# Attention in segments: behind each score run either transposes or products with v

## Chip, cores and metric

The kernel runs on one core of one Trainium2 chip. The metric is the device time of one execution in microseconds (us); lower is better. The engines are called by their names in the profile: PE (TensorE, with PEld for its weight loads), DVE (VectorE), ACT (ScalarE), POOL (GpSimd) and SP (SyncE, whose queue issues the transfers).

## What is computed

The reference is attention with a bias from relative positions, and two feed-forward stages behind it. The change concerns the attention alone:

```python
B, H, S, D = q.shape                       # 4, 8, 576, 64
scores = scale * np.matmul(q, k.transpose(0, 1, 3, 2))
...
scores = scores + bias.transpose(2, 0, 1)[None, :, :, :]
scores = scores - np.max(scores, axis=-1, keepdims=True)
attn = np.exp(scores)
attn = attn / (np.sum(attn, axis=-1, keepdims=True) + 1e-09)
return np.matmul(attn, v).astype(np.float32)
```

Its output, 2304 tokens of 512 values, goes through `(h * cos(h)) @ w_out` with `h = x @ w_in`, then through a normalized gated stage. Those two stages are the same before and after the change.

## The kernel before

The order of the instructions is written out by hand: the schedule is manual, and each engine works through its own queue in program order. The program has three stretches. Up to about 60 us the bias is computed and stored. Up to about 308 us there is the attention. Then come the items of the two feed-forward stages (`run_item`), which use PE almost alone.

The attention is a loop over 16 units u, four batches b for each of four pairs of heads hp, and in each unit over five steps p (`step(u, p)`). A step p < 4 takes 128 queries of both heads, and p = 4 takes the last 64 queries of both heads at once. The work of one unit is:

- **Scores** (`qk`): each operand is split in two parts, and three products of parts make one score. For p < 4 the two heads lie on the two row halves of the array, which gives 12 matmuls on two PSUM tiles `psS`. For p = 4 there are 6 matmuls on one tile over all rows. `psS` has two buffers.
- **Softmax**: `most` (DVE) adds the bias, finds the largest score and writes `e` to SBUF. `exps` (ACT) makes the exponential in place and its sum. For the ninth tile (p = 4) a small POOL copy fills up 64 columns of `e` behind the exponential. `e` has three buffers, one for each step.
- **Transposes** (`tr`): `e` is transposed on PE in blocks of 128 columns into PSUM tiles `pt` (three buffers). ACT or DVE copies each tile into `eT` in SBUF. There is one `eT` for the first 256 queries (half 0) and one for the other 320 (half 1), each with one buffer. A step p < 4 has 9 transposes and p = 4 has 5.
- **Products with v** (`av`): for each half, five blocks c of keys, each with the two heads on the two column halves of the array, gathered in one PSUM tile `o` (one buffer). A product shows as two matmul records.
- **Normalization**: `recip` (DVE) inverts the sums, and a POOL copy widens them to `rw`. `norm` transposes `rw` on PE (two transposes) and copies the result to `rbc`. `norm_out` multiplies `o` by it (DVE), rounds it to `xh` (ACT) and stores the rest `xl` (POOL).

The units overlap. In step p of unit u the transposes belong to step p - 2 of the same unit, or to p + 3 of the unit before. The products belong to the unit before: half 0 at p = 0 (blocks 0 to 2) and p = 1 (blocks 3, 4), half 1 at p = 2 and p = 3. So PE runs scores, transposes and products in each of p = 0 to 3, and scores and transposes at p = 4. `recip` of half 1 stands at the end of p = 0 and its `rw` is transposed at p = 2. `recip` of half 0 stands at the end of p = 2 and its `rw` is transposed at p = 4. `norm_out` stands at the head of p = 2 and p = 4.

Side work goes along. `split_k` and `split_q` (POOL, a cast and a subtraction for each block) split the operands of the next unit: k at p = 2, blocks 0 and 1 of q at p = 3, blocks 2 and 3 at p = 4, and block 4 at p = 0 of the unit that uses it. From unit 4 on, `w_conv` (DVE, four quarters for each piece) and `w_tick` (ACT, POOL and the transfers) prepare weights for the later stages.

Of the kernel before, what the change touches and what calls it, by code (L numbers as in the profile page):

```python
# [7 lines left out]
F32 = mybir.dt.float32  # L8
# [7 lines left out]
B, H, S, D = 4, 8, 576, 64  # L16
# [15 lines left out]
WA = 1  # L32
WB = 6
# [21 lines left out]
def attn_moe(tc, qd, kd, vd, smallp, lrow, ident_d, wf1, wf2, rmsg, out):  # L55
    nc = tc.nc
# [23 lines left out]
    ident = const.tile([128, 128], F32, name="ident")  # L80
# [5 lines left out]
    psA, st_psA = pool("psA", space=PSUM, side="left")  # L86
# [96 lines left out]
    def load(u):  # L183
        for k, src in enumerate((kd, qd)):
            if u == 0:
                t = rawp.tile([128, 512, 2], I32, tag="raw", name="first", bufs=NRAW)
                t = t.rearrange("p a b -> p (a b)")[:, 0:640].bitcast(F32)
            else:
                t = prep.tile([128, 640], F32, tag="raw" + "kq"[k], name="raw" + "kq"[k], bufs=1)
            nc.sync.dma_start(t, src[u % 4, u // 4])  # L190
            raw_kq[u, k] = t
        if u == 0:
            kq[0] = [raw_kq[0, 0], raw_kq[0, 1]]
# [10 lines left out]
    def split_q(u, p):  # L204
        c = slice(128 * p, 128 * p + 128)
        two_parts(qt_[:, :, c], raw_kq[u, 1][:, c])
# [19 lines left out]
    ap, st_ap = pool("att")  # L226
# [3 lines left out]
    st = {}  # L230

    def qk(u, p):


        kt, qt = kq[u]
        terms = TERMS
        if u == 0:
            terms, kt, qt = ((0, 0),), kt.unsqueeze(1), qt.unsqueeze(1)
        pss = [psB.tile([128, 2, 512], F32, tag="S", name="psS", bufs=2) for _ in range(2 if p < 4 else 1)]
        for x in range(2):  # L240
            for n, (a, b_) in enumerate(terms):
                for hh, ps in enumerate(pss):
                    r = slice(64 * hh, 64 * hh + 64) if p < 4 else slice(0, 128)
                    k0 = 64 - 64 * hh + 288 * x
                    nc.tensor.matmul(ps[:, x, 0:288], qt[r, a, 128 * p:128 * p + 128], kt[r, b_, k0:k0 + 288],  # L245
                                     start=(n == 0), stop=(n == len(terms) - 1), tile_position=(64 * hh, 0))
        return pss

    def softmax(u, j, ps):
        most(u, j, ps)  # L250
        exps(u, j)
# [17 lines left out]
        if j == 8:  # L269
            nc.gpsimd.tensor_copy(e2[:, S:S + 64], e2[:, S - 64:S])  # L270

    def tr(u, p, first, spread=None):
        s_ = st[u]
        if first and p in (0, 2):
            s_["eT", p // 2] = ap.tile([128, 9, 256 + 32 * p], F32, tag=f"eT{p}", name=f"eT{p}", bufs=1)
        e = s_["e"][p]
        eT, q0 = s_["eT", min(p // 2, 1)], 128 * (p % 2 if p < 4 else 2)
        n = 128 if p < 4 else 64
        pt = psA.tile([128, 512], F32, tag="tr", name="pt", bufs=3)
        if first:  # L280
            for i in range(4):
                k0 = 128 * (i // 2) + (S + 64) * (i % 2) if p < 4 else 128 * i
                nc.tensor.transpose(pt[:, 128 * i:128 * i + 128], e[:, k0:k0 + 128], ident)  # L283
            nc.scalar.copy(eT[:, 0:512 // n, q0:q0 + n], pt.rearrange("p (c q) -> p c q", q=n))
            return
        if p < 4:
            for i in range(4):
                k0 = 128 * (2 + i // 2) + (S + 64) * (i % 2)
                nc.tensor.transpose(pt[:, 128 * i:128 * i + 128], e[:, k0:k0 + 128], ident)  # L289
            nc.vector.tensor_copy(eT[:, 4:8, q0:q0 + n], pt.rearrange("p (c q) -> p c q", q=n))  # L290
            pt = psA.tile([128, 512], F32, tag="tr", name="pt", bufs=3)
        nc.tensor.transpose(pt[:, 0:128], e[:, 512:640], ident)  # L292
        if spread is not None:
            norm(*spread, pt[:, 128:384])
        if p < 4:
            nc.scalar.copy(eT[:, 8, q0:q0 + n], pt[:, 0:128])
        else:
            for r in (slice(0, 64), slice(64, 128)):
                nc.vector.tensor_copy(eT[r, 8, q0:q0 + n], pt[r, r])
        del s_["e"][p]  # L300

    def av(u, half, cs):
        s_ = st[u]
        n = 256 if half == 0 else 320
        eT = s_["eT", half]
        if cs[0] == 0:
            s_["o"] = psA.tile([128, 512], F32, tag="o", name="o", bufs=1)
        o = s_["o"]
        if half == 1 and cs[0] == 0:
            for hh in range(2):  # L310
                nc.tensor.matmul(o[64 * hh:64 * hh + 64, 320:384], s_["r"][:, 8:9].to_broadcast([128, 64]),
                                 ident[:, 64 * hh:64 * hh + 64], start=True, stop=True, tile_position=(0, 64 * hh))
        vt = vts[u]
        for c in cs:
            for hh in ((0, 1) if c % 2 else (1, 0)):
                nc.tensor.matmul(o[64 * hh:64 * hh + 64, 0:n], vt[:, c, 64 * hh:64 * hh + 64],  # L316
                                 eT[:, 2 * c + (hh if c < 4 else 0), :], start=(c == 0), stop=(c == 4),
                                 tile_position=(0, 64 * hh))
# [3 lines left out]
    def recip(u, half):  # L322
        s_ = st[u]
        a, z = (0, 4) if half == 0 else (4, 9)
        nc.vector.tensor_scalar(s_["sum"][:, a:z], s_["sum"][:, a:z], 1e-9, None, op0=ALU.add)
        nc.vector.reciprocal(s_["r"][:, a:z], s_["sum"][:, a:z])
        s_["rw"] = ap.tile([128, 320], F32, tag="rbc", name="rw", bufs=2)
        nc.gpsimd.tensor_copy(s_["rw"][:, 0:256].rearrange("p (a b) -> p a b", b=64),
                              s_["r"][:, a:a + 4].unsqueeze(2).to_broadcast([128, 4, 64]))

    def norm(u, half, rp):
        s_ = st[u]
        rw = s_.pop("rw")
        for i in range(0, 256, 128):
            nc.tensor.transpose(rp[:, i:i + 128], rw[:, i:i + 128], ident)
        rbc = ap.tile([128, 320], F32, tag="rbc", name="rbc", bufs=2)
        nc.scalar.copy(rbc[:, 0:256], rp)
        s_["rbc", half] = rbc

    def norm_tail(u):  # L340
        s_ = st[u]
        nc.scalar.copy(s_["rbc", 1][:, 256:320], s_["o"][:, 320:384])

    def norm_out(u, half):
        hp, b = divmod(u, 4)
        s_ = st[u]
        n = 256 if half == 0 else 320
        rbc = s_["rbc", half]
        xt = ap.tile([128, 320], F32, tag="xt", name="xt", bufs=1)
        nc.vector.tensor_tensor(xt[:, 0:n], s_["o"][:, 0:n], rbc[:, 0:n], op=ALU.mult)  # L350
        t0 = b * S + 256 * half
        nc.scalar.copy(xh[:, hp, t0:t0 + n], xt[:, 0:n])
        nc.gpsimd.tensor_tensor(xl[:, hp, t0:t0 + n], xt[:, 0:n], xh[:, hp, t0:t0 + n].bitcast(F32), op=ALU.subtract)

    def start_unit(u):
# [6 lines left out]
            "m": sm[:, 0:9], "sum": sm[:, 10:19], "r": sm[:, 20:29], "e": {},  # L362
        }

    def step(u, p):
        hp, b = divmod(u, 4)
        if p == 0:
            start_unit(u)
        if u > 0 and p in (2, 4):
            norm_out(u - 1, p // 4)  # L370
        pss = qk(u, p)

        if p == 3 and u > 0:
            norm_tail(u - 1)
        back = (u, p - 2) if p > 1 else (u - 1, p + 3)
        if back[0] >= 0:
            tr(*back, True)
        for j, ps in enumerate(pss, 2 * p):
            softmax(u, j, ps)
            if b == 3:  # L380
                load_bias(hp + 1, j)
        if back[0] >= 0:
            tr(*back, False, (u, 0) if p == 4 else (u - 1, 1) if p == 2 and u > 0 else None)
        if p == 2:
            recip(u, 0)
        if p == 0 and u > 0:
            recip(u - 1, 1)
        if p < 4 and u > 0:
            av(u - 1, p // 2, ([0, 1, 2], [3, 4])[p % 2])
        if p == 0 and u > 1:  # L390
            split_q(u, 4)
        if 0 < u < 15:
            if p == 0:
                load(u + 1)
            if p == 2:
                split_k(u + 1)
            if p > 2:
                split_q(u + 1, 2 * p - 6)
                split_q(u + 1, 2 * p - 5)
        if u >= 4 and p != 2:  # L400
            if wstate["conv"] < wstate["absd"]:
                w_conv(1)
            if p == 4:
                w_tick(lambda i: i < WA + WB)

    ph0, st_ph0 = pool("ph0", side="right")
    L = ph0.tile([128, S], F32, name="L")
# [349 lines left out]
            w_fill(2 if n % 2 else 1)  # L757

    def rest():
        norm_out(15, 0)  # L760
        av(15, 1, [0, 1, 2, 3, 4])
        norm_tail(15)

    tr(15, 3, True)
    tr(15, 3, False)
    recip(15, 1)
    av(15, 0, [0, 1, 2, 3, 4])
    tr(15, 4, True)
    tr(15, 4, False, (15, 1))
    run_item(0, rest)  # L770
    run_item(1, lambda: norm_out(15, 1))
    st_psA.close()
# [79 lines left out]
```

## Time and profile before

| | |
|---|---|
| median of 3 runs | 1167.45 us (1166.16 to 1167.52) |
| the profiled execution's own time | 1166.25 us |
| its span, first to last instruction | 1164.5 us |
| PE busy | 1148.8 us |
| DVE, ACT, POOL busy | 811.5, 548.2, 442.5 us |

The profile is one execution. Busy time of PE is matmul time with modelled ends, so neighbours overlap by a little; the distance from start to start tells what a matmul takes in a row of its kind. An engine that is not the bottleneck may idle without cost.

### The profile page before, as it was taken

To read this page: it belongs to the slowest core of one execution; us is meant where nothing else is said; L and a number is where in the kernel's file an instruction comes from. 1 tells how busy PE (TensorE), PEld (TensorE's weight loads), DVE (VectorE), ACT (ScalarE), POOL (GpSimd) and SP (SyncE) were. 2 spreads that over 40 slices of the span, in tenths; PEclk is the share of its full clock that TensorE was granted. 3 is DMA by queue.
4 is the path that set the end of the run, shared out by engine and by line. 5 is a ranking of instruction groups with operands and counts; after the bars stand their busy time and mean duration, and the time that the engine had idled before them with its cause. 6 is when DMAs were issued, how large, how long until landed. Compare 5 with 4: busy or idle time off the path is not lost.

```text
span 1164.5 us, 18515 instructions
## 1 busy us (share of the span) xinstructions
PE 1148.8 (99%) x6962; PEld 912.8 (78%) x6962; DVE 811.5 (70%) x1524; ACT 548.2 (47%) x1122; POOL 442.5 (38%) x554
## 2 busy tenths in 40 slices
PE   7999999999999999999999999999999999999998
PEld 3477777777788888888888878888888888888887
DVE  8866678888698799698879897874655255543232
ACT  7977778888554454445444546332222232222111
POOL 0235556566242352244234356653321242133111
PEclk9999999999999999999999999999999999999999
DMA  6924343442111011111101100220112011100011
GB/s 217 315 79 149 105 145 117 144 148 78 33 55 55 1 55 55 37 37 55 55 19 55 37 19 19 59 69 19 43 54 68 1 55 55 55 1 1 37 55 72
DMA packets 30713, 79.27 MB, mean 68 GB/s; under 512 B 3872, under 2 KB 4128, under 8 KB 30624
## 3 DMA queue, kind: packets, MB, share of 16 engines
q1 hardware_dynamic: 30480, 77.80, 21.1%
q8 instruction: 55, 0.90, 0.3%
q10 hardware_dynamic: 144, 0.29, 0.1%
q14 instruction: 34, 0.28, 0.1%
HBM read 62.47 MB, written 15.61 MB: 67 GB/s over the span
## 4 chain that ended last, share of the span: by engine, by line
PE 87%; DVE 8%; ACT 3%; issue 1%; DMA 1%; SPq 0%; POOL 0%; DVEq 0%; ACTq 0%
PE y L552 25%; PE h L552 14%; PE hg L552 12%; PE hv L552 12%; PE o L316 7%; PE psS L245 7%; PE pt L283 4%; PE pt L289 2%; PE psb L475 2%; ACT G L484 1%; DVE yacc L655 1%; PE pt L292 1%; DVE t L592 1%; DVE sq L671 1%; DVE w L128 1%
## 5 line engine op out<-in xcount | busy, mean ns | idle before, releaser
L602 POOL TENSOR_TENSOR g<-t,g 128x512 fp32r<-128x512 f32 (+1 forms) x80 | 98.4, 1230 | 234.5 <-ACT g L601 234.5
L619 POOL TENSOR_TENSOR g<-t,g 128x512 fp32r<-128x512 f32 (+1 forms) x60 | 74.4, 1240 | 292.1 <-ACT g L618 292.1
L259 DVE CUSTOM_DVE_ANT_0 e<-psS,bias 128x576 f32<-128x576 f32 x144 | 104.0, 755 | 52.0 <-PE psS L245 49.8
L552 PE MATMUL y<-g,wB 128*128 128x512 f32 (+1 forms) x600 | 133.4, 370 | 1.3 <-DVE yacc L655 1.2
L614 DVE TENSOR_TENSOR t<-t,hg 128x512 f32<-128x512 f32 (+1 forms) x60 | 38.0, 633 | 137.5 <-ACT t L613 137.5
L552 PEld LDWEIGHTS y<-g,wB 128*128 128x128 f32 x600 | 105.0, 188 | 21.6 <-DVE yacc L655 2.5
L613 ACT ACTIVATE t<-hg 128x512 f32<-128x512 f32 (+1 forms) x60 | 33.2, 554 | 167.3 <-PE hg L552 161.0
L618 ACT CAST g<-t 128x512 fp32r<-128x512 f32 (+1 forms) x60 | 34.7, 578 | 164.3 <-DVE t L617 164.3
L268 ACT ACTIVATE e<-e,sm 128x576 f32<-128x576 f32 x144 | 110.7, 773 | 1.2 <-DVE sm L259 1.2
L552 PE MATMUL h<-xh,wB 128*128 128x512 f32 (+1 forms) x360 | 109.1, 369 | 0.0
L552 PE MATMUL hg<-xh,wB 128*128 128x512 f32 (+1 forms) x320 | 96.9, 368 | 0.4 <-DVE t L614 0.4
L552 PE MATMUL hv<-xh,wB 128*128 128x512 f32 (+1 forms) x320 | 97.1, 369 | 0.0
L596 ACT ACTIVATE r<-r 128x512 f32<-128x512 f32 (+1 forms) x80 | 47.1, 589 | 106.0 <-DVE r L593 105.7
L601 ACT CAST g<-t 128x512 fp32r<-128x512 f32 (+1 forms) x80 | 46.2, 578 | 96.8 <-DVE t L600 87.6
L552 PE MATMUL y<-wB,g 128*128 128x512 f32 x378 | 91.4, 389 | 0.0
L316 PE MATMUL o<-eT,v 128*64 128x256 f32 (+1 forms) x640 | 90.5, 413 | 0.0
L245 PEld LDWEIGHTS psS<-kt,qt 64*128 64x128 f32 (+1 forms) x810 | 62.0, 185 | 29.4 <-issue 20.3
L552 PEld LDWEIGHTS y<-wB,g 128*128 128x128 f32 x378 | 70.5, 188 | 14.3
L245 PE MATMUL psS<-kt,qt 64*128 64x288 f32 (+1 forms) x810 | 79.8, 309 | 0.4 <-DVE sm L259 0.4
L552 PE MATMUL y<-g,wC 128*128 128x512 f32 (+1 forms) x360 | 79.8, 370 | 0.1
L617 DVE TENSOR_TENSOR t<-t,hv 128x512 f32<-128x512 f32 (+1 forms) x60 | 38.0, 633 | 58.5 <-PE hv L552 58.4
L552 PEld LDWEIGHTS h<-xh,wB 128*128 128x128 f32 x360 | 65.8, 188 | 12.1 <-issue 0.5
(136 smaller groups left out, 2663.7 us busy)
## 6 DMA issues: line engine op xcount, KB each, us to landing
raw<-in_wf_dram SPq DMA_DIRECT2D x68, 512.0 KB, 3.6
bdram<-G SPq DMA_DIRECT2D x36, 295.5 KB, 4.8
bias<-bdram SPq DMA_DIRECT2D x32, 288.0 KB, 4.3
v<-in_vd_dram SPq DMA_DIRECT2D x16, 320.0 KB, 4.7
rawk<-in_kd_dram SPq DMA_DIRECT2D x15, 320.0 KB, 5.0
rawq<-in_qd_dram SPq DMA_DIRECT2D x15, 320.0 KB, 3.6
out_dram<-yacc SPq DMA_DIRECT2D x16, 256.0 KB, 2.0
bias<-bdram SPq DMA_DIRECT2D x4, 144.0 KB, 2.9
```

Of the source, the lines that this page charges most:

```text
L245: nc.tensor.matmul(ps[:, x, 0:288], qt[r, a, 128 * p:128 * p + 128], kt[r, b_, k0:k0 + 288], start=(n == 0), stop=(n == len(terms) - 1), t ...
L259: nc.vector.tensor_tensor_reduce(out=e.rearrange("p (a b) -> p a b", a=2), in0=ps[:, :, 0:288], in1=bias_t[j].rearrange("p (a b) -> p a b" ...
L268: nc.scalar.activation(e, e, AF.Exp, bias=s_["m"][:, j:j + 1], scale=-1.0, accum_out=s_["sum"][:, j:j + 1])
L283: nc.tensor.transpose(pt[:, 128 * i:128 * i + 128], e[:, k0:k0 + 128], ident)
L316: nc.tensor.matmul(o[64 * hh:64 * hh + 64, 0:n], vt[:, c, 64 * hh:64 * hh + 64], eT[:, 2 * c + (hh if c < 4 else 0), :], start=(c == 0), s ...
L552: nc.tensor.matmul(ps, a, b_, start=(first and k == 0), stop=(last and k == tot - 1))
L596: nc.scalar.activation(r, r, AF.Abs)
L601: nc.scalar.copy(g[:, 0, :tn], t)
L602: nc.gpsimd.tensor_tensor(g[:, 1, :tn], t, g[:, 0, :tn].bitcast(F32), op=ALU.subtract)
L614: nc.vector.tensor_tensor(t, t, pg, op=ALU.mult)
L617: nc.vector.tensor_tensor(t, t, pv, op=ALU.mult)
L619: nc.gpsimd.tensor_tensor(g[:, 1, :tn], t, g[:, 0, :tn].bitcast(F32), op=ALU.subtract)
```

## The change

`step` is written anew. Behind the scores of p = 0, 2 and 4 stand only transposes, and behind those of p = 1 and 3 only products with v:

- p = 0: all transposes of steps 3 and 4 of the unit before (w = u - 1), and of its `rw` of half 1 (`turn_end`);
- p = 1: all products of half 1 of w, and its `norm_out`;
- p = 2: all transposes of steps 0 and 1 of u, and of its `rw` of half 0;
- p = 3: all products of half 0 of u, and its `norm_out`;
- p = 4: all transposes of step 2 of u.

`tr` becomes `blocks` (four transposes into one `pt`) and `ninths` (the ninth blocks of up to two steps, and `rw`, in one `pt`). They return their copies, which `step` puts between the exponentials. `norm` goes into `ninths`. `recip` of half 1 moves from the end of p = 0 to the end of p = 4, behind the `split_q` of that step, and `recip` of half 0 from p = 2 to p = 1. The weight quarters move from one each at p = 0, 1, 3 and 4 to two each at p = 1 and p = 3, and `w_tick` from p = 4 to p = 1. The places of `split_k` and `split_q` stay.

```diff
--- before.py
+++ after.py
@@ -269,49 +269,59 @@
         if j == 8:
             nc.gpsimd.tensor_copy(e2[:, S:S + 64], e2[:, S - 64:S])
 
-    def tr(u, p, first, spread=None):
+    def blocks(u, p, k):
         s_ = st[u]
-        if first and p in (0, 2):
+        if k == 0 and p in (0, 2):
             s_["eT", p // 2] = ap.tile([128, 9, 256 + 32 * p], F32, tag=f"eT{p}", name=f"eT{p}", bufs=1)
         e = s_["e"][p]
         eT, q0 = s_["eT", min(p // 2, 1)], 128 * (p % 2 if p < 4 else 2)
         n = 128 if p < 4 else 64
         pt = psA.tile([128, 512], F32, tag="tr", name="pt", bufs=3)
-        if first:
-            for i in range(4):
-                k0 = 128 * (i // 2) + (S + 64) * (i % 2) if p < 4 else 128 * i
-                nc.tensor.transpose(pt[:, 128 * i:128 * i + 128], e[:, k0:k0 + 128], ident)
-            nc.scalar.copy(eT[:, 0:512 // n, q0:q0 + n], pt.rearrange("p (c q) -> p c q", q=n))
-            return
-        if p < 4:
-            for i in range(4):
-                k0 = 128 * (2 + i // 2) + (S + 64) * (i % 2)
-                nc.tensor.transpose(pt[:, 128 * i:128 * i + 128], e[:, k0:k0 + 128], ident)
-            nc.vector.tensor_copy(eT[:, 4:8, q0:q0 + n], pt.rearrange("p (c q) -> p c q", q=n))
-            pt = psA.tile([128, 512], F32, tag="tr", name="pt", bufs=3)
-        nc.tensor.transpose(pt[:, 0:128], e[:, 512:640], ident)
-        if spread is not None:
-            norm(*spread, pt[:, 128:384])
-        if p < 4:
-            nc.scalar.copy(eT[:, 8, q0:q0 + n], pt[:, 0:128])
-        else:
-            for r in (slice(0, 64), slice(64, 128)):
-                nc.vector.tensor_copy(eT[r, 8, q0:q0 + n], pt[r, r])
-        del s_["e"][p]
-
-    def av(u, half, cs):
+        for i in range(4):
+            k0 = 128 * (2 * k + i // 2) + (S + 64) * (i % 2) if p < 4 else 128 * i
+            nc.tensor.transpose(pt[:, 128 * i:128 * i + 128], e[:, k0:k0 + 128], ident)
+        to = eT[:, 4 * k:4 * k + 512 // n, q0:q0 + n]
+        return lambda copy: copy(to, pt.rearrange("p (c q) -> p c q", q=n))
+
+    def ninths(u, ps, half=None):
+        s_ = st[u]
+        pt = psA.tile([128, 512], F32, tag="tr", name="pt", bufs=3)
+        for i, p in enumerate(ps):
+            nc.tensor.transpose(pt[:, 128 * i:128 * i + 128], s_["e"].pop(p)[:, 512:640], ident)
+        if half is not None:
+            rw = s_.pop("rw")
+            for i in range(0, 256, 128):
+                nc.tensor.transpose(pt[:, 256 + i:384 + i], rw[:, i:i + 128], ident)
+
+        def out(copy):
+            if ps[0] == 0:
+                copy(s_["eT", 0][:, 8, 0:256], pt[:, 0:256])
+            else:
+                q0 = 128 * (ps[0] - 2)
+                copy(s_["eT", 1][:, 8, q0:q0 + 128], pt[:, 0:128])
+
+        def small(copy):
+            for r0 in (0, 64):
+                r = slice(r0, r0 + 64)
+                copy(s_["eT", 1][r, 8, 256:320], pt[r, 128 + r0:192 + r0])
+
+        def spread():
+            rbc = ap.tile([128, 320], F32, tag="rbc", name="rbc", bufs=2)
+            nc.scalar.copy(rbc[:, 0:256], pt[:, 256:512])
+            s_["rbc", half] = rbc
+        return out, small, spread
+
+    def av(u, half):
         s_ = st[u]
         n = 256 if half == 0 else 320
         eT = s_["eT", half]
-        if cs[0] == 0:
-            s_["o"] = psA.tile([128, 512], F32, tag="o", name="o", bufs=1)
-        o = s_["o"]
-        if half == 1 and cs[0] == 0:
+        o = s_["o"] = psA.tile([128, 512], F32, tag="o", name="o", bufs=1)
+        if half == 1:
             for hh in range(2):
                 nc.tensor.matmul(o[64 * hh:64 * hh + 64, 320:384], s_["r"][:, 8:9].to_broadcast([128, 64]),
                                  ident[:, 64 * hh:64 * hh + 64], start=True, stop=True, tile_position=(0, 64 * hh))
         vt = vts[u]
-        for c in cs:
+        for c in range(5):
             for hh in ((0, 1) if c % 2 else (1, 0)):
                 nc.tensor.matmul(o[64 * hh:64 * hh + 64, 0:n], vt[:, c, 64 * hh:64 * hh + 64],
                                  eT[:, 2 * c + (hh if c < 4 else 0), :], start=(c == 0), stop=(c == 4),
@@ -327,15 +337,6 @@
         s_["rw"] = ap.tile([128, 320], F32, tag="rbc", name="rw", bufs=2)
         nc.gpsimd.tensor_copy(s_["rw"][:, 0:256].rearrange("p (a b) -> p a b", b=64),
                               s_["r"][:, a:a + 4].unsqueeze(2).to_broadcast([128, 4, 64]))
-
-    def norm(u, half, rp):
-        s_ = st[u]
-        rw = s_.pop("rw")
-        for i in range(0, 256, 128):
-            nc.tensor.transpose(rp[:, i:i + 128], rw[:, i:i + 128], ident)
-        rbc = ap.tile([128, 320], F32, tag="rbc", name="rbc", bufs=2)
-        nc.scalar.copy(rbc[:, 0:256], rp)
-        s_["rbc", half] = rbc
 
     def norm_tail(u):
         s_ = st[u]
@@ -362,46 +363,84 @@
             "m": sm[:, 0:9], "sum": sm[:, 10:19], "r": sm[:, 20:29], "e": {},
         }
 
+    def turn_end(u, *now):
+        a, b, c = blocks(u, 3, 0), blocks(u, 3, 1), blocks(u, 4, 0)
+        out, small, spread = ninths(u, (3, 4), 1)
+        a(nc.scalar.copy)
+        if now:
+            exps(now[0], 0)
+        c(nc.scalar.copy)
+        b(nc.vector.tensor_copy)
+        out(nc.scalar.copy)
+        small(nc.vector.tensor_copy)
+        if now:
+            exps(now[0], 1)
+        spread()
+
+    def convert(n):
+        for _ in range(n):
+            if wstate["conv"] < wstate["absd"]:
+                w_conv(1)
+
     def step(u, p):
         hp, b = divmod(u, 4)
+        w = u - 1
         if p == 0:
             start_unit(u)
-        if u > 0 and p in (2, 4):
-            norm_out(u - 1, p // 4)
-        pss = qk(u, p)
-
-        if p == 3 and u > 0:
-            norm_tail(u - 1)
-        back = (u, p - 2) if p > 1 else (u - 1, p + 3)
-        if back[0] >= 0:
-            tr(*back, True)
-        for j, ps in enumerate(pss, 2 * p):
-            softmax(u, j, ps)
+        for j, ps in enumerate(qk(u, p), 2 * p):
+            most(u, j, ps)
             if b == 3:
                 load_bias(hp + 1, j)
-        if back[0] >= 0:
-            tr(*back, False, (u, 0) if p == 4 else (u - 1, 1) if p == 2 and u > 0 else None)
-        if p == 2:
+        if p == 0:
+            turn_end(w, u)
+            if u > 1:
+                split_q(u, 4)
+            if u < 15:
+                load(u + 1)
+        elif p == 1:
+            if w >= 0:
+                av(w, 1)
+            exps(u, 2)
+            exps(u, 3)
+            if u >= 4:
+                convert(2)
+                w_tick(lambda i: i < WA + WB)
             recip(u, 0)
-        if p == 0 and u > 0:
-            recip(u - 1, 1)
-        if p < 4 and u > 0:
-            av(u - 1, p // 2, ([0, 1, 2], [3, 4])[p % 2])
-        if p == 0 and u > 1:
-            split_q(u, 4)
-        if 0 < u < 15:
-            if p == 0:
-                load(u + 1)
-            if p == 2:
+            if w >= 0:
+                norm_tail(w)
+                norm_out(w, 1)
+        elif p == 2:
+            cs = [blocks(u, i, k) for i in range(2) for k in range(2)]
+            out, _, spread = ninths(u, (0, 1), 0)
+            cs[0](nc.scalar.copy)
+            cs[1](nc.scalar.copy)
+            exps(u, 4)
+            cs[2](nc.vector.tensor_copy)
+            cs[3](nc.vector.tensor_copy)
+            out(nc.scalar.copy)
+            exps(u, 5)
+            spread()
+            if 0 < u < 15:
                 split_k(u + 1)
-            if p > 2:
-                split_q(u + 1, 2 * p - 6)
-                split_q(u + 1, 2 * p - 5)
-        if u >= 4 and p != 2:
-            if wstate["conv"] < wstate["absd"]:
-                w_conv(1)
-            if p == 4:
-                w_tick(lambda i: i < WA + WB)
+        elif p == 3:
+            av(u, 0)
+            exps(u, 6)
+            exps(u, 7)
+            if u >= 4:
+                convert(2)
+            norm_out(u, 0)
+        else:
+            c0, c1 = blocks(u, 2, 0), blocks(u, 2, 1)
+            out, _, _ = ninths(u, (2,))
+            c0(nc.scalar.copy)
+            exps(u, 8)
+            c1(nc.vector.tensor_copy)
+            out(nc.scalar.copy)
+        if 0 < u < 15 and p > 2:
+            split_q(u + 1, 2 * p - 6)
+            split_q(u + 1, 2 * p - 5)
+        if p == 4:
+            recip(u, 1)
 
     ph0, st_ph0 = pool("ph0", side="right")
     L = ph0.tile([128, S], F32, name="L")
@@ -757,16 +796,10 @@
             w_fill(2 if n % 2 else 1)
 
     def rest():
-        norm_out(15, 0)
-        av(15, 1, [0, 1, 2, 3, 4])
+        av(15, 1)
         norm_tail(15)
 
-    tr(15, 3, True)
-    tr(15, 3, False)
-    recip(15, 1)
-    av(15, 0, [0, 1, 2, 3, 4])
-    tr(15, 4, True)
-    tr(15, 4, False, (15, 1))
+    turn_end(15)
     run_item(0, rest)
     run_item(1, lambda: norm_out(15, 1))
     st_psA.close()
```

## Rows read from the trace of the kernel before

**Rows 1.** The page, part 1: busy us, share of the span and instructions.
```profile
PE 1148.8 (99%) x6962; PEld 912.8 (78%) x6962; DVE 811.5 (70%) x1524; ACT 548.2 (47%) x1122; POOL 442.5 (38%) x554
```
**Rows 2.** Busy us by stretch: length, PE, PEld, DVE, ACT, POOL, granted clock, DMA, GB/s.
```profile
124.00:301.00 177.00, 177.00 (x1580) 127.79 (x1577) 142.59 (x370) 141.32 (x372) 102.13 (x191) 1.00 0.36 116
301.70:304.60 2.90, 2.85 (x24) 2.22 (x23) 2.37 (x5) 2.59 (x7) 1.22 (x2) 1.00 0.01 3
```
**Rows 3.** Chain of waits in order of time: start, us, what; scores of p = 4.
```profile
252.87 0.99 PE psS L245 x6
...
300.95 0.99 PE psS L245 x6
```
**Rows 4.** Timeline of PE: start, us, line, operation, tiles, shapes, count.
```profile
236.78 1.06 PE L245 MATMUL psS<-kt,qt 128*128 128x288 f32 x6
237.68 0.60 PE L283 MATMUL pt<-ident,e 128*128 128x128 f32 x4
...
238.98 1.07 PE L245 MATMUL psS<-kt,qt 64*128 64x288 f32 x12
239.97 0.65 PE L283 MATMUL pt<-ident,e 128*128 128x128 f32 x4
240.46 0.60 PE L289 MATMUL pt<-ident,e 128*128 128x128 f32 x4
240.90 0.27 PE L292 MATMUL pt<-ident,e 128*128 128x128 f32 x1
241.10 1.52 PE L316 MATMUL o<-eT,v 128*64 128x256 f32 x12
242.55 1.05 PE L245 MATMUL psS<-kt,qt 64*128 64x288 f32 x12
...
304.56 2.38 PE L316 MATMUL o<-eT,v 128*64 128x256 f32 x20
306.87 0.66 PE L283 MATMUL pt<-ident,e 128*128 128x128 f32 x4
```
**Rows 5.** Timeline of DVE and ACT at a step p = 4.
```profile
237.88 0.76 DVE L259 CUSTOM_DVE_ANT_0 e<-psS,bias 128x576 f32<-128x576 f32 x1 [0.30 <-PE psS L245]
...
238.37 0.58 ACT L284 COPY eT<-pt 128x512 f32<-128x512 f32 x1 [0.29 <-PE pt L283]
...
238.86 0.78 ACT L268 ACTIVATE e<-e,sm 128x576 f32<-128x576 f32 x1
...
239.53 0.19 ACT L268 ACTIVATION_READ_ACCUMULATOR e<-e,sm 128x1 f32 x1
```
**Rows 6.** Groups by line and form, 60 to 308 us: busy us, mean ns, idle before.
```profile
L328 POOL COPY rw<-sm 128x256 f32<-128x256 f32 x31 | 12.6, 405 | 33.3 <-DVE sm L326 33.3
...
L353 POOL TENSOR_TENSOR xl<-xt,xh 128x256 fp32r<-128x256 f32 x15 | 11.0, 733 | 41.7 <-ACT xh L352 41.7
...
L325 DVE TENSOR_SCALAR sm<-sm 128x5 f32<-128x5 f32 x16 | 7.8, 489 | 0.0
...
L350 DVE TENSOR_TENSOR xt<-o,rbc 128x256 f32<-128x256 f32 x15 | 6.4, 425 | 0.5
...
L352 ACT CAST xh<-xt 128x256 fp32r<-128x256 f32 x15 | 6.0, 401 | 0.7
...
L326 DVE RECIPROCAL sm<-sm 128x5 f32<-128x5 f32 x16 | 3.1, 191 | 0.6
```
**Rows 7.** Timeline of POOL, from the copy of e on.
```profile
239.79 0.35 POOL L270 COPY e<-e 128x64 f32<-128x64 f32 x1 [0.76 <-ACT e L268]
240.08 0.29 POOL L196 CAST qt<-rawq 128x128 fp32r<-128x128 f32 x1
...
240.86 0.29 POOL L196 CAST qt<-rawq 128x128 fp32r<-128x128 f32 x1
...
241.64 1.28 POOL L149 TENSOR_TENSOR wB<-w,wB 128x512 fp32r<-128x512 f32 x1
```
**Rows 8.** One line, 60 to 308 us: duration in ns, min/median/max, first and last start.
```profile
L197 POOL TENSOR_TENSOR qt<-rawq,qt x70: 453/458/847, 75.7 to 291.4; 128x128 fp32r<-128x128 f32 x70
```

## The prediction

> **What bounds the kernel now.** I read the page's busy times first. TensorE (PE) is busy for 1148.8 of 1164.5 us, so only PE time counts, unless a wait is put into its order [rows 1]. Then the table by stage: in the steady part of the attention (124 to 301 us) PE is busy all the time at the full granted clock (1.00, the level of 2.4 GHz), with VectorE (DVE) at 142.6, ScalarE (ACT) at 141.3 and GpSimd (POOL) at 102.1 of 177 us [rows 2]. Then the chain of waits in order of time: it stays on PE, and the scores of p = 4 start three units apart at 252.87 and 300.95, which makes 16.03 us a unit [rows 3]. The last view is PE's timeline, which shows what fills those 16.03 us: score runs (S), runs of transposes (T) and runs of products with v (A), each a little longer than its matmuls [rows 4].
>
> The price of a run, from [rows 4]. Four transposes inside a T run take 240.90 - 240.46 = 0.44, so 0.109 each. The first four take 0.49 (0.05 for entering) and the last one 0.20 up to the first product (0.09 for leaving): a T run costs 0.109 for each transpose and a constant of 0.15. Only the T run behind p = 4 enters free (11 transposes, 237.68 to 238.98, 1.30, constant 0.10). For A, 12 matmul records of 256 columns take 1.45 and 20 take 2.31, so a pair takes 0.215 and the constant is 0.16; I use 0.15, the T constant, for both. An S run takes 0.99, and 0.90 at p = 4.
>
> **What the change takes away.** Work on PE is the same: 45 transposes and 20 products (40 records) a unit, 5 S runs. The number of runs falls. Before, T follows each of five S runs and A follows four of the T runs: 9 runs of T or A. After, T stands behind p = 0 (16 transposes), p = 2 (20) and p = 4 (9), A behind p = 1 and p = 3: 5 runs. Two T constants and two A constants go: 4 x 0.15 = 0.60 us a unit. The S runs keep theirs, whatever stands next to them. This holds for units 1 to 15; unit 0 has as many changes of kind as before, and the last stretch before the first item of the next stage comes out about even when its waits are followed through. 15 x 0.60 = 9.0 us.
>
> S directly before A does not occur in the trace. Its lowest price is that of any other change (0.15, already counted in the run), its highest that of the S-to-T and T-to-A changes which it replaces, one constant more. Then 2 x 0.15 a unit come back and the gain is 4.5 us. I take the low price: the two constants that the trace has, of T behind S and of A behind T, are nearly the same. The Trainium skill (TensorEngine Tiling (Array Packing), Key Properties) says that changing the tiling mode drains TensorE. By that rule S to A is one drain like the others, which is the low price, and the sum is the same.
>
> Smaller edits: three ACT copies of 128 columns where there were four (one of them twice as wide), and the conversion quarters moved from four steps to two. ACT and DVE have 20% of the steady part free [rows 2], so these count as nothing; if that cover went, PE would see it only where a product run waits for a copy. Followed through p = 0 to p = 3 with durations like those of [rows 5, 6], the copies come at least 0.1 us ahead of the run that needs them, and the transposes' three PSUM buffers are freed in time. The DMA issues are as many as before and go ahead of their use by several steps.
>
> **What the change adds: a wait on POOL.** Before, the widened reciprocals rw of unit u-1 were made at p = 0 and transposed at p = 2. Now recip(u, 1) stands at the end of p = 4, and its transposes close the T run of the next p = 0. POOL works in the order written, and between the last products of unit u and this rw stand ten POOL instructions: the subtraction xl of norm_out(u, 0), moved to p = 3; split_q for blocks 0 and 1; the small copy of e behind exps(u, 8); split_q for blocks 2 and 3. Then rw. norm_out(u, 0) cannot start before the last product of p = 3. (split_k, at p = 2, is done by then.)
>
> I set the start of the p = 4 scores to zero. The products' records end 0.07 after the next S starts [rows 4]. DVE's product takes 0.425, ACT's cast 0.401, the subtraction 0.733 [rows 6]; a hand-over between engines takes 0.07, as from ACT's last record (239.53 + 0.19) to POOL's copy at 239.79 [rows 5, 7]. So xl ends at 0.07 + 0.07 + 0.425 + 0.07 + 0.401 + 0.07 + 0.733 = 1.84. Two split_q take 241.64 - 240.08 = 1.56 [rows 7], so 3.40. The copy of e holds POOL for 240.08 - 239.79 = 0.29, so 3.69; its own input is ready earlier: most(u, 8) starts 1.10 after S4's start and takes 0.76 (236.78 and 237.88), the ACT copy ahead of exps starts 0.69 after T's start, at 1.59, exps follows 0.49 later and its last record ends 0.86 after that, at 2.94 [rows 4, 5]. Two more split_q: 5.25. rw takes 0.405 [rows 6]: 5.66, and 0.07 to PE: 5.73.
>
> PE without a wait: S4 0.90, nine transposes 9 x 0.109 + 0.10 = 1.08, S0 0.99, then 14 transposes, 14 x 0.109 + 0.05 = 1.58: the transposes of rw are due at 4.55. They come 5.73 - 4.55 = 1.18 us late. Part of it is spent sooner: the scores of p = 0 need split_q's block 0, which ends at about 1.84 + 0.78 + 0.07 = 2.69, and were due at 1.98, so PE waits about 0.7 there and about 0.5 at rw. Behind rw on PE everything is queued, S of p = 1 first. split_q is issued in p > 2 only for 0 < u < 15, so 14 units pay: 14 x 1.18 = 16.5 us.
>
> Bounds of this stall. Below: the pitch from xl to the next POOL instruction could be 0.05 shorter than its duration, as the copy's is, which gives 1.13; nothing in the order written lets rw pass the eight split instructions, so I see no reason for less than 0.85, a quarter below. Above: one of the four subtractions slowed from 0.458 to 0.847, its median and its maximum in the attention [rows 8], gives 1.57.
>
> **Sum.** -9.0 + 16.5 = +7.5 us on the profiled run, whose own time is 1166.25 (span 1164.5): 1173.8. The median of the runs shown is 1.2 higher, 1167.45, which gives 1175.0. I predict 1174, between the low end of the stall and this sum.
>
> **Rivals.**
> *Faster: POOL is not late.* The place is the head of S0 and the end of T at p = 0. It decides below a stall of 9.0 / 14 = 0.64 us a unit, so the POOL chain would have to be 0.5 us shorter than the 5.7 that I add up. For it: the page itself calls POOL's spans rough. Against: the 1.56 are start to start, in a stretch where POOL never idled. If POOL were on time, DVE would be next: recip waits for exps(u, 8) (2.94), then takes 0.489 and 0.191 [rows 6], so most(u+1, 0) would start at about 3.65 and the second one end at 3.65 + 2 x 0.76 = 5.17, where S1 was due at 2.97 + 16 x 0.109 + 0.15 = 4.86. That is a stall of 0.3 a unit, 4.5 us in all, and 1166.25 - 4.5 = 1161.7 (1163 by the median). With no stall at all: 1157.3 (1158.5).
>
> *No change.* The stall lies near break-even, 0.5 to 0.8: 1165 to 1170. It needs the chain to be 0.4 to 0.7 shorter than added up.
>
> *Slower still.* S to A costs twice and a subtraction of POOL is slowed in each unit: -4.5 + 14 x 1.57 = +17.5, 1184.
>
> *The clock falls.* From 301.7 to 304.6 PE did little but transposes, with gaps, and the granted clock stayed at 1.00 [rows 2]. If it fell to half behind each of the three T runs for one S run, 3 x 0.99 x 15 = 45 us would be lost: 1211. The Trainium skill (TensorE: Matmul & The Clock Gate, Part 4) says that transposes do not count as busy for the clock in the way matmuls do. By that rule the longer T runs speak for this rival; the trace, with 1.00 through its densest stretch of transposes, does not bear it out.
>
> **How the numbers follow.** Forecast, a stall of 0.85 to 1.5 (1170 to 1180): 0.68. Slower still: 0.08. The clock: 0.02. No change: 0.08. Faster: 0.14. About 0.2% is what a measurement of this kernel can tell from no change, 2.3 us. That gives slower 0.78, same 0.08, faster 0.14. The likeliest case alone spans 1170 to 1180. The range reaches down to 1163, the faster case with DVE's wait, and up to 1183; about 0.08 lie below it and 0.04 above.
>
> **What would show it.** In the profile after: S runs of p = 0 and p = 1 whose weight loads wait for POOL, together about 1.2 us a unit; POOL without a pause from xl to rw; 16.6 us from one p = 4 to the next; five T and A runs a unit with unbroken 16 and 20 transposes, and 20 records of products; no wait of PE on the eT copies; the clock at 1.00. The prediction is wrong if rw's transposes follow the other fourteen at 0.109, if S0 starts 0.20 behind the last transpose of p = 4, or if PE waits for DVE or ACT at the product runs instead.

## The result, and the profile after

The changed kernel takes 1173.68 us (median of 6 runs, 1172.76 to 1174.08); the kernel before, measured beside it, 1166.85 us. The ratio is 1.0059 with a 95% interval of 1.0049 to 1.0070: slower by about 7 us. The forecast was 1174. The profiled execution took 1173.41 us with a span of 1171.6 us, 7.1 more than before.

The table by stage of the kernel after (length, then busy us of PE, PEld, DVE, ACT and POOL, the granted clock, DMA):

```profile
124.00:301.00 177.00, 171.49 (x1521) 125.22 (x1519) 135.91 (x357) 137.37 (x348) 97.26 (x191) 1.00 0.37 114
```

In [rows 2] PE was busy in all of these 177 us; now it idles for 5.5 of them by its records, and the clock is as it was. The waits from 76 to 310 us (who waited for whom: us in total, times, longest) say for what:

```profile
PEld pt L294 <- POOL rw L338: 8.2, 14, 0.6
...
PEld psS L245 <- DVE sm L335: 6.9, 14, 0.5
...
PEld psS L245 <- POOL qt L196: 5.3, 14, 0.4
...
PEld psS L245 <- POOL qt L197: 3.4, 14, 0.2
```

Each stands 14 times. In the three that name POOL, the transposes of rw wait for its copy, and the scores of p = 0 wait for both halves of a split_q block. The one that names DVE (`recip`) stands at the scores of p = 2 and costs PE nothing: the scores there start at 254.11, 0.08 before the record of the products in front of them ends (251.32 + 2.87), as scores behind products do in [rows 4] (0.07). So an idle weight load need not be a loss, and these sums are more than PE's own loss. The loss is read from PE's timeline, from one p = 4 through the next p = 1:

```profile
240.93 1.06 PE L245 MATMUL psS<-kt,qt 64*128 64x288 f32 x12
241.92 2.38 PE L326 MATMUL o<-eT,v 128*64 128x256 f32 x20
244.23 1.06 PE L245 MATMUL psS<-kt,qt 128*128 128x288 f32 x6
245.13 1.04 PE L282 MATMUL pt<-ident,e 128*128 128x128 f32 x8
246.00 0.27 PE L290 MATMUL pt<-ident,e 128*128 128x128 f32 x1
246.41 1.34 PE L245 MATMUL psS<-kt,qt 64*128 64x288 f32 x12
247.68 1.53 PE L282 MATMUL pt<-ident,e 128*128 128x128 f32 x12
249.05 0.40 PE L290 MATMUL pt<-ident,e 128*128 128x128 f32 x2
249.80 0.44 PE L294 MATMUL pt<-ident,rw 128*128 128x128 f32 x2 [0.35 <-POOL rw L338]
250.17 1.05 PE L245 MATMUL psS<-kt,qt 64*128 64x288 f32 x12
...
255.09 2.11 PE L282 MATMUL pt<-ident,e 128*128 128x128 f32 x16
...
257.62 1.06 PE L245 MATMUL psS<-kt,qt 64*128 64x288 f32 x12
```

The weight loads of the scores of p = 0 show which half of the block they wait for (L196 is the cast, L197 the subtraction):

```profile
246.41 0.30 PEld L245 LDWEIGHTS psS<-kt,qt 64*128 64x128 f32 x4 [0.37 <-POOL qt L196]
246.95 0.56 PEld L245 LDWEIGHTS psS<-kt,qt 64*128 64x128 f32 x8 [0.25 <-POOL qt L197]
```

The scores of p = 0 start 0.41 behind the last transpose of p = 4, where 0.20 is usual ([rows 4]): 0.21 lost. They last 1.27 and not 0.99: 0.28 lost inside the run, since its first matmuls need only the cast half of the block and the later ones the subtracted half. rw's transposes start at 249.80; 0.109 behind the second ninth block would be 249.27: 0.53 lost. Together 1.02 us.

POOL's timeline of the same stretch, from xl to rw:

```profile
245.39 0.73 POOL L354 TENSOR_TENSOR xl<-xt,xh 128x256 fp32r<-128x256 f32 x1 [2.82 <-ACT xh L353]
246.07 0.29 POOL L196 CAST qt<-rawq 128x128 fp32r<-128x128 f32 x1
...
247.62 0.24 POOL L270 COPY e<-e 128x64 f32<-128x64 f32 x1
247.79 0.30 POOL L196 CAST qt<-rawq 128x128 fp32r<-128x128 f32 x1
...
249.35 0.40 POOL L338 COPY rw<-sm 128x256 f32<-128x256 f32 x1
```

After xl nothing on POOL waits any more: ten instructions run back to back, and rw is the last of them.

The chain of waits in order of time passes through them too. At the next unit's rw it reads (start, us, what):

```profile
266.10 0.35 POOL rw L338
...
266.49 0.44 PE pt L294 x2
```

From one unit's transposes of rw to the next one's are 266.49 - 249.80 = 16.69 us; [rows 3] gave 16.03 for a unit.

### The profile page after: what moved, and what is told of

It reads as the page before. It is cut to its first block, busy times and chain, and to the rows that moved or that the text cites. A ratio compares the mean times of both kernels' runs of the same rounds, so it can differ in the third digit from the quotient of the medians.

```text
span 1171.6 us, 18397 instructions
## 1 busy us (share of the span) xinstructions
PE 1148.8 (98%) x6962; PEld 914.8 (78%) x6962; DVE 809.3 (69%) x1524; ACT 550.3 (47%) x1106; POOL 435.5 (37%) x554
## 4 chain that ended last, share of the span: by engine, by line
PE 78%; DVE 9%; ACT 6%; POOL 5%; issue 2%; DMA 1%; POOLq 0%; ACTq 0%; DVEq 0%
PE y L591 25%; PE h L591 14%; PE hg L591 12%; PE hv L591 12%; PE psS L245 5%; PE o L326 4%; PE pt L282 3%; POOL qt L197 2%; PE psb L514 2%; ACT e L268 2%; POOL qt L196 1%; DVE yacc L694 1%; ACT G L523 1%; POOL xl L354 1%; PE pt L294 1%
## 5 line engine op out<-in xcount | busy, mean ns | idle before, releaser
L245 PE MATMUL psS<-kt,qt 64*128 64x288 f32 (+1 forms) x810 | 83.1, 312 | 2.1
L326 PE MATMUL o<-eT,v 128*64 128x256 f32 (+1 forms) x640 | 83.9, 408 | 0.0
L591 PEld LDWEIGHTS y<-wB,g 128*128 128x128 f32 x378 | 70.5, 188 | 14.3
```

The source lines that it names most:

```text
L591: nc.tensor.matmul(ps, a, b_, start=(first and k == 0), stop=(last and k == tot - 1))
```

## The experiments

Four kernels move nothing but split_q and recip about in the changed kernel, so that rw comes earlier or later. All times are medians; the kernel before gave 1166.55 beside these four.

**rw ahead of blocks 2 and 3.**

```diff
-        if 0 < u < 15 and p > 2:
-            split_q(u + 1, 2 * p - 6)
-            split_q(u + 1, 2 * p - 5)
         if p == 4:
             recip(u, 1)
+        if 0 < u < 15 and p > 2:
+            split_q(u + 1, 2 * p - 6)
+            split_q(u + 1, 2 * p - 5)
```

> At p = 4 the reciprocals (recip and the POOL copy rw) are written ahead of the split_q of blocks 2 and 3; all else as in the changed kernel. Theory (POOL's order makes rw late): rw is free of two split_q (1.56 us), so the wait of 0.56 us at the transposes of rw goes and the 0.49 at the scores of p = 0 stays: 14 x 0.56 = 7.8 us less, about 1166. Rival (DVE's recip and the two most behind it bind next): they would be due 0.3 us after PE without stalls, which the 0.49 still hides, so also 1166. Rival (the loss comes from the scores standing directly before the products, or from the PSUM buffers): no change, 1173.7.

Measured: 1166.66 us. PE's timeline:

```profile
241.35 0.27 PE L290 MATMUL pt<-ident,e 128*128 128x128 f32 x1
241.76 1.34 PE L245 MATMUL psS<-kt,qt 64*128 64x288 f32 x12
...
244.40 0.41 PE L290 MATMUL pt<-ident,e 128*128 128x128 f32 x2
244.64 0.38 PE L294 MATMUL pt<-ident,rw 128*128 128x128 f32 x2
```

The wait at rw is gone (0.24 behind the ninth blocks, which is two transposes), and the wait at the scores of p = 0 is left as it was, 0.41 and a run of 1.27.

**Blocks 0 and 1 ahead of norm_out.**

```diff
         elif p == 3:
+            if 0 < u < 15:
+                split_q(u + 1, 0)
+                split_q(u + 1, 1)
             av(u, 0)
...
-        if 0 < u < 15 and p > 2:
-            split_q(u + 1, 2 * p - 6)
-            split_q(u + 1, 2 * p - 5)
+        if 0 < u < 15 and p == 4:
+            split_q(u + 1, 2)
+            split_q(u + 1, 3)
```

> At p = 3 the split_q of blocks 0 and 1 are written ahead of norm_out; all else as in the changed kernel. Theory: the wait at the scores of p = 0 (0.49 us) goes; POOL then starts the copy of e when exps(u, 8) ends, and rw comes 0.65 us late instead of 0.56, so the stall falls from 1.05 to 0.65: 14 x 0.40 = 5.6 us less, about 1168. If POOL's order is not the cause: 1173.7.

Measured: 1167.79 us. The other half of the pattern:

```profile
242.15 0.27 PE L290 MATMUL pt<-ident,e 128*128 128x128 f32 x1
242.35 1.07 PE L245 MATMUL psS<-kt,qt 64*128 64x288 f32 x12
...
244.71 0.41 PE L290 MATMUL pt<-ident,e 128*128 128x128 f32 x2
245.50 0.44 PE L294 MATMUL pt<-ident,rw 128*128 128x128 f32 x2 [0.38 <-POOL rw L338]
```

The scores start 0.20 behind the transposes and last 0.99; rw is 0.57 late.

**Both moves.** At p = 3 as in the second, at p = 4 recip ahead of blocks 2 and 3 as in the first.

> Both moves together. Theory with POOL as the only cause: the whole stall of 14 x 1.05 = 14.7 us goes, 1159. Rival that DVE is next (recip waits for exps(u, 8), the two most of p = 0 come behind it, and the scores of p = 1 wait for them): 0.3 us a unit stay, about 1163. If neither: 1173.7.

Measured: 1159.65 us, 14.0 less than the changed kernel and a ratio of 0.9943 (0.9929 to 0.9957) to the kernel before. Both waits are gone:

```profile
204.24 0.27 PE L290 MATMUL pt<-ident,e 128*128 128x128 f32 x1
204.44 1.07 PE L245 MATMUL psS<-kt,qt 64*128 64x288 f32 x12
...
206.80 0.40 PE L290 MATMUL pt<-ident,e 128*128 128x128 f32 x2
207.04 0.38 PE L294 MATMUL pt<-ident,rw 128*128 128x128 f32 x2
207.35 1.06 PE L245 MATMUL psS<-kt,qt 64*128 64x288 f32 x12
```

From p = 4's scores, at 202.46, to rw's transposes are 4.58 us. The rival that DVE binds next fell: the scores of p = 1 follow without a wait.

**One split_q more ahead of rw.** The dose the other way.

```diff
             split_q(u + 1, 2 * p - 5)
+            if p == 4:
+                split_q(u + 1, 4)
...
-            if u > 1:
-                split_q(u, 4)
```

> The split_q of block 4, which stands at p = 0 behind the transposes, is moved to p = 4 of the unit before, ahead of rw; the work is the same. Theory: rw comes one split_q later, 0.78 us in each of 14 units: 10.9 us more, about 1184.6. If POOL's order is not the cause: 1173.7.

Measured: 1183.99 us, 10.3 more. In those 14 units the run of transposes at p = 0, with rw's at its end, takes 3.23 to 3.26 where it took 2.49 (247.68 to 250.17) in the changed kernel. With both moves, the changed order and one block more, the time follows what stands on POOL ahead of rw.

The version with both moves still waits in one place, at p = 2 of the units that split weights. There 20 transposes end 2.71 after their start, against 2.41 in the other units. ACT's timeline in that version:

```profile
211.04 0.60 ACT L148 CAST wB<-w 128x512 fp32r<-128x512 f32 x1
211.55 0.66 ACT L113 ACTIVATE w<-raw 128x512 f32<-128x512 f32 x1
212.12 0.18 ACT L343 COPY rbc<-o 128x64 f32<-128x64 f32 x1
212.93 0.46 ACT L353 CAST xh<-xt 128x320 fp32r<-128x320 f32 x1 [0.63 <-DVE xt L351]
213.29 1.07 ACT L284 COPY eT<-pt 128x512 f32<-128x512 f32 x2
```

The weight work stands ahead of the copy of rbc, DVE's xt waits for that copy, ACT for xt, and the eT copies of p = 2 come behind. Two kernels remove this in different ways (1166.90 for the kernel before, beside them).

**Weight work at p = 3.**

```diff
         elif p == 1:
...
                 convert(2)
-                w_tick(lambda i: i < WA + WB)
...
         elif p == 3:
...
                 convert(2)
+                w_tick(lambda i: i < WA + WB)
             norm_out(u, 0)
```

> On the kernel with both moves (1159.65): w_tick goes from p = 1 to p = 3, ahead of norm_out. Theory: in the units with a weight split ACT's two weight instructions (1.1 us) stand ahead of the copy of rbc, DVE's xt and ACT's xh, so the first eT copies of p = 2 are late and the transposes of p = 2 take 2.71 where they take 2.41 otherwise; at p = 3 ACT idles, so the 0.3 us go in some 7 units: 2.1 us less, about 1157.5. Rival: at p = 3 they delay xh and with it the copies of p = 4 and p = 0 by as much: 1159 to 1160.

Measured: 1157.82 us. The 20 transposes of p = 2 take 2.40 or 2.41 in every unit.

**norm_tail ahead of the weight work.**

```diff
+            if w >= 0:
+                norm_tail(w)
             if u >= 4:
                 convert(2)
                 w_tick(lambda i: i < WA + WB)
             recip(u, 0)
             if w >= 0:
-                norm_tail(w)
                 norm_out(w, 1)
```

> On the kernel with both moves (1159.65): at p = 1 the small copy norm_tail is written ahead of the weight work, which stays at p = 1. Theory: xt no longer waits for the copy (0.7 to 0.95 us), the weight work fills ACT's wait for xt, and xh and the eT copies come in time: 2.1 us less, about 1157.5. Rival: ACT is simply full in p = 1, whatever the order: no change, 1159.6.

Measured: 1157.74 us, a ratio of 0.9923 (0.9911 to 0.9935) to the kernel before. ACT after that move:

```profile
211.77 0.21 ACT L343 COPY rbc<-o 128x64 f32<-128x64 f32 x1 [0.29 <-PE o L326]
211.87 0.62 ACT L148 CAST wB<-w 128x512 fp32r<-128x512 f32 x1
212.40 0.67 ACT L113 ACTIVATE w<-raw 128x512 f32<-128x512 f32 x1
212.97 0.45 ACT L353 CAST xh<-xt 128x320 fp32r<-128x320 f32 x1
```

The weight work now fills the time in which ACT waited for xt, and the 20 transposes take 2.40 (212.63 to 215.03 on PE). By these runs neither of the two is faster than the other (1157.82 and 1157.74), and they were not tried together. The second was measured once more beside the next kernel:

> The kernel with both moves and norm_tail first once more, beside the one with a run more: 1157.7 by all theories.

Measured: 1157.97 us (1166.35 for the kernel before).

The last question is the gain: is it the number of runs, at 0.15 us each? Two kernels put one run of each kind back.

**One run more at p = 3.**

```diff
-            av(u, 0)
+            av(u, 0, [0, 1, 2])
+            c0 = blocks(u, 2, 0)
+            av(u, 0, [3, 4])
             exps(u, 6)
             exps(u, 7)
+            c0(nc.scalar.copy)
...
-            c0, c1 = blocks(u, 2, 0), blocks(u, 2, 1)
+            c1 = blocks(u, 2, 1)
             out, _, _ = ninths(u, (2,))
-            c0(nc.scalar.copy)
```

> On the kernel with both moves and norm_tail first (1157.7): the first four transposes of step 2 are taken out of the run at p = 4 and written between the third and the fourth block of the products at p = 3, so that each unit has one run of transposes and one of products more; the work is the same. Theory (a run costs a constant of 0.15 us, whatever its neighbours): 2 x 0.15 us in each of 16 units, 4.8 us more, about 1162.5. Rival (the gain of the segments comes from other things, such as fewer copies or the weight work moved): no change, 1157.7.

Measured: 1168.59 us, 10.6 more than the 1157.97 beside it: more than twice the 4.8 of the theory, where the rival gave none. PE's timeline shows two parts:

```profile
205.40 1.52 PE L328 MATMUL o<-eT,v 128*64 128x256 f32 x12
206.85 0.66 PE L282 MATMUL pt<-ident,e 128*128 128x128 f32 x4
207.44 1.08 PE L328 MATMUL o<-eT,v 128*64 128x256 f32 x8
...
209.35 0.60 PE L282 MATMUL pt<-ident,e 128*128 128x128 f32 x4
...
209.98 1.43 PE L245 MATMUL psS<-kt,qt 64*128 64x288 f32 x12
211.35 1.53 PE L282 MATMUL pt<-ident,e 128*128 128x128 f32 x12
```

The products of p = 3 take 1.45 + 1.01, where one run takes 2.31: 0.15 more. The four transposes take 0.59, four times 0.109 and 0.15. That is the 0.30 that was expected. But the scores of p = 0 last 1.37 and not 0.99. Their weight loads, in the same stretch:

```profile
209.98 0.18 PEld L245 LDWEIGHTS psS<-kt,qt 64*128 64x128 f32 x1 [0.17 <-issue]
210.37 0.81 PEld L245 LDWEIGHTS psS<-kt,qt 64*128 64x128 f32 x11 [0.20 <-DVE sm L259]
```

The second one waits for most (DVE) of p = 4: the run at p = 4 now takes 0.63 and no longer covers the time until DVE frees the score tile. 0.38 more, 0.68 in all, 10.2 us in 15 units.

**One run more at p = 1.** The same at a place with nothing to cover.

```diff
-                av(w, 1)
+                av(w, 1, [0, 1, 2])
+            s0 = blocks(u, 0, 0)
+            if w >= 0:
+                av(w, 1, [3, 4])
             exps(u, 2)
             exps(u, 3)
+            s0(nc.scalar.copy)
...
-            cs = [blocks(u, i, k) for i in range(2) for k in range(2)]
+            cs = [None, blocks(u, 0, 1), blocks(u, 1, 0), blocks(u, 1, 1)]
             out, _, spread = ninths(u, (0, 1), 0)
-            cs[0](nc.scalar.copy)
```

> On the kernel with both moves and norm_tail first (1157.7): the first four transposes of p = 2 (step 0, first block) are taken out of that run and written between the third and the fourth block of the products at p = 1, their ACT copy behind exps(u, 3); the work is the same. The run before lost 0.68 us a unit, of which 0.30 were the two constants and 0.38 a wait of the scores of p = 0 for psS, because the run at p = 4 had become too short to cover most(u, 8); the run at p = 2 is long enough that this can't happen. Theory: 2 x 0.15 us more in 15 units, less the 0.08 us by which the run at p = 2 now waits for its PSUM buffers: 3.3 to 4.5 us, 1161 to 1162. Rival (what a run more costs is mostly the waits that it sets off elsewhere): as before 10 us, 1168, or none.

Measured: 1161.96 us, 4.2 more than the 1157.74 of the version that it was made from.

```profile
212.30 0.66 PE L282 MATMUL pt<-ident,e 128*128 128x128 f32 x4
212.89 1.30 PE L328 MATMUL o<-eT,v 128*64 128x320 f32 x8
214.12 1.06 PE L245 MATMUL psS<-kt,qt 64*128 64x288 f32 x12
```

Four transposes take 0.59 again, and eight product records of 320 columns 1.23, as they did in the kernel before.

## Why the prediction was right

**The bound and the runs.** Right. PE sets the time, and a run of transposes or products costs a constant of 0.15 us: both kernels with a run more show it, and the second lost 4.2 us by little else: 0.15 a unit for the products and 0.10 for the transposes, whose run at p = 2 waits 0.05 less for a PSUM buffer, some 4 us in 16 units. What the segments gave, with the waits gone, is read from the units of the version with both moves and norm_tail first: from unit 1 on, one p = 4 to the next takes 15.51 to 15.54 there, about 0.5 less than the 16.03 before. That is the 0.60 of the forecast less what the covers below took back. S directly before A costs the low price: the scores of p = 3 take 0.99 (240.93 to 241.92) and the products behind them 2.31, the same as in [rows 4] behind transposes. That agrees with the sentence of the Trainium skill (TensorEngine Tiling (Array Packing), Key Properties) that changing the tiling mode drains TensorE: scores of p < 4, transposes and products stand in the profile with three different tiles (`64*128`, `128*128`, `128*64`), and the products cost the same behind either of the other two.

**The wait on POOL.** Right in its place, its cause and its parts. With the start of p = 4's scores at zero (244.23), forecast and measured: split_q of block 0 starts at 1.84 and 1.84, the copy of e at 3.40 and 3.39, block 2 at 3.69 and 3.56, rw at 5.25 and 5.12, its transposes on PE at 5.73 and 5.57; without a wait they are due at 4.55, and the version with both moves has them at 4.58. The stall is 1.02 us and not 1.18. The difference is mostly the copy of e, which holds POOL for 0.17 where [rows 7] gave 0.29. In 14 units that is 14.3 us and not 16.5. Both moves together gave back 14.0, although the transposes of p = 2 take 0.2 more in seven units of that version (2.71 where the changed kernel has 2.50 to 2.53).

**The first wait.** Half right. About 0.7 was forecast at the head of the scores of p = 0, and 0.49 came, 0.28 of it inside the run: the first matmuls need the cast half of the block alone, which the forecast did not use. The 0.2 spared there is no gain, because rw sets the end: it would have come at rw on top of the 0.5, had POOL's chain not been 0.16 shorter than forecast, and so 0.53 came there. For the same reason it was the transposes of rw that waited for POOL behind p = 0, and not the scores of p = 1, which the forecast named as a sign.

**The covers.** The PSUM buffers were said to be freed in time. They are not quite: the 20 transposes of p = 2 take 2.40 to 2.53 (2.53 from 255.09 to 257.62), where 20 x 0.109 + 0.15 is 2.33, so 0.07 to 0.20 a unit, about 2.0 us over 16 units (their sum is 39.3, and 16 x 2.33 is 37.3). The larger figures stand in the seven units that split weights, and the two versions that order the weight work otherwise have 2.40 or 2.41 throughout: that part comes from the weight work moved to p = 1, which the forecast counted as nothing. That the other 0.08 is a wait for a buffer is in part argued: the profile names ACT's copy as the releaser in four units only. This was the term left out. In the changed kernel it nearly makes up for the smaller stall: -9.0 + 14.3 + 2.0 = +7.3, against 7.1 in the spans. So the mechanism was right, but that 1174 came within 0.4 us of the median is partly luck: a stall 2.2 us too long and a term of 2.0 us left out cancelled each other.

**The rivals.** Faster with POOL on time: POOL was late, so the condition did not hold. Where the two moves made it hold, the time came out at 1159.65, near the 1158.5 given for no stall at all and not the 1163 given for a wait on DVE. That wait did not come: the forecast took 0.489 for recip's first instruction, a mean over the kernel before; in the changed kernel its median is 0.170 and its longest 0.172. S to A at twice the price: not so. The clock: 1.00 over the stretch with all its runs of 20 transposes, and 1.00 inside one of them (255.10 to 257.50), so the rule of the Trainium skill (TensorE: Matmul & The Clock Gate, Part 4), by which transposes do not count as busy for the clock in the way matmuls do, does not show here.

## What to carry to other kernels

When a step is moved later, follow it through the in-order queue of every engine that it uses, the slow one too: a saving of some 0.5 us a unit on the engine that sets the time was lost to a chain of ten instructions on POOL (1.02 us a unit), although POOL was idle for more than a third of the stretch. Then look at the order before giving the change up: the same segments with two split_q moved ahead and the reciprocals put before two others are 0.57% faster than the kernel before, and 0.77% with one small copy moved as well. A run of matmuls may also cover another engine's release of a buffer; what is cut from it must leave that cover.

## What was not expected

A score run did not wait for its whole operand. Where split_q was late, the run started when the cast half was there and waited again 0.28 us inside for the subtracted half; a wait of that kind shows as a run of 1.27 in place of 0.99, with little idle time ahead of it. And shortening the run at p = 4 by four transposes cost more (0.38 us a unit) than the two run changes that were the experiment's purpose (0.30).
